# Wider value steps and single-element projections, a shorter inverse root, one more kept value tile an element, and a swapped softmax in a four-element transformer decode

## The chip, the cores and the metric

The kernel runs on one core of a Trainium2 chip. The metric is the time of one execution in device microseconds (us), lower is better. Single executions of this kernel differ by up to 4% on a busy chip, so each kernel is timed several times, alternating with the kernel before on the same chip.

## The reference, cut to what matters

Four batch elements, one query token each. Two identical layers, each attention over a cache of 4,096 keys and values, then a feed-forward network (FFN) with GELU. Both layers read the same key and value caches: 8 key/value heads of 4,096 x 128 in bf16, each serving 4 query heads.

```python
B, Sq, D = 4, 1, 512
Hq, Hkv, Sk, Dh = 32, 8, 4096, 128
F = 1792
x = x + attention(layernorm(x), k_cache, v_cache, wq, wo)
x = x + (gelu(layernorm(x) @ w_gate) * (layernorm(x) @ w_up)) @ w_down
# ... and the same two lines once more
```

Keys and values together are 67 MB for each sweep over all elements. The keys of an element stay on the chip from its first layer to its second; most value tiles have to be loaded twice.

## The kernel before

Elements are numbered 0 to 3. Each goes through the same round: key tiles (512 KB each) are loaded and scored, softmax runs on ScalarE and VectorE, value tiles pass through seven buffers, and a "dense stage" (output projection, FFN, query of the next layer) ends the element's first layer. The second layer's scores then free the key tiles, and the next element's keys are loaded into them. `vals.step()` is one value step: sixteen matmuls on one value tile, after which its buffer is free and the next load is issued.

```python
WIDE = 8                         # how often the four probabilities are streamed
...
# one value step: 4 neighbouring elements (the 4 query heads), repeated WIDE times
rhs = pe[:, s, c, :].unsqueeze(1).broadcast_to([P, WIDE, rep])
nc.tensor.matmul(self.ot[:, s % 2], lhsT=v[:, i, :], rhs=rhs, ...)
if last or (b, g, s, t) not in keep:
    free.append(held.pop((b, g, s, t)))
load_v()
...
# FFN down projection: ONE element (nb = 1), repeated n = 32 times
def down(nb, H_bf, between=()):
    n = WIDE * rep // nb
    y = ps_sm.tile([P, KD, n, nb], FP32, name="y", tag="sm")
    ...
            nc.tensor.matmul(y[:, k], lhsT=wd_sb[:, c, k * P:(k + 1) * P],
                             rhs=H_bf[:, c, :].unsqueeze(1).broadcast_to([P, n, nb]), ...)
    return y[:, :, 0]            # only the first copy is used
...
# projection of the last heads: one element, one column
nc.tensor.matmul(y[:, k], lhsT=wo_sb[:, i, k * P:(k + 1) * P], rhs=head_rhs(o_bf, i), ...)
...
# softmax and value steps at the start of an element's attention
p0 = soft(sc1)
vals.step(3)
soft_turn(p0)                    # VectorE transposes the probabilities
if not first:
    for i in range(2):
        out_proj(rows, OT_bf, heads[i], hp, i == 0)
pe, den = soft_swap(p0, p1p), soft_den(p0)     # TensorE turns them once more
...
# which value tiles stay on the chip for the second layer: some of element 0
keep = {(0,) + u[2:] for u in value_order(0, 1)[:KEEP]}
```

The repeated columns compute nothing new. They are there for TensorE's clock: in the first series below, doubling them in the value steps alone took the mean granted clock of the profiled run from 0.741 to 0.868.

## Time and profile before

| | kernel before |
|---|---|
| time, median of 3 runs | 308.94 us (307.83 to 309.42) |
| span of the profiled run | 306.7 us |
| data on the queue | 113.53 MB, busy 94.9% of the span |
| key loads start (elements 1, 2, 3), and the last refill of key tiles | 88.48, 146.78, 210.41, 274.34 us |
| mean granted TensorE clock | 0.741 |

From the profile's page: busy time of each engine, and the clock that was granted in 40 equal slices of the span, in tenths.

```profile
PE 202.7 (66%) x3865; PEld 119.6 (39%) x3873; DVE 172.6 (56%) x490; ACT 29.3 (10%) x71; POOL 0.7 (0%) x6
...
PEclk9999995556778559795976567889855585678675
```

No engine is busy all the time, and the clock changes between half (5) and full (9) about once a dense stage. The groups of instructions show the down projection, with its count, its busy time and the mean duration of one:

```profile
L356 PE MATMUL y<-H_bf,wd_sb 128*128 128x32 bf16 x280 | 9.6, 192 | 3.4 <-DVE H_bf L340 1.7
```

The durations of matmuls that follow each other overlap, so 192 ns is not the price of one. What a matmul costs in a dense sequence is the distance from one start to the next, which I computed from the trace for each group and each clock state. At full clock the down matmuls start 31 ns apart and the value matmuls, which stream as many columns, 25 ns apart.

### The profile page before, as it was taken

How to read it: one execution, taken by the hardware profiler on the slowest of the kernel's cores; microseconds unless marked ns; L12 is line 12 of the kernel's file. 1: busy time of each engine (PE TensorE's matmuls, PEld its weight loads, DVE VectorE, ACT ScalarE, POOL GpSimd, SP SyncE). 2: the span in 40 equal slices, each digit the busy share in tenths (PEclk: the TensorE clock that was granted, in tenths of full speed). 3: DMA queues.
4: the chain of work that ended last, by engine and by line, in shares of the span. 5: the costliest groups of instructions: out<-in, count | busy, mean ns of one | idle time of the engine just before them, and what ended most of it. 6: DMA issues, size and time to landing. Idle time of an engine off the chain costs nothing.

```text
span 306.7 us, 8771 instructions
## 1 busy us (share of the span) xinstructions
PE 202.7 (66%) x3865; PEld 119.6 (39%) x3873; DVE 172.6 (56%) x490; ACT 29.3 (10%) x71; POOL 0.7 (0%) x6
## 2 busy tenths in 40 slices
PE   1344385348786657889854379797563868997974
PEld 0011154122333134656431236474311455645654
DVE  6586831014358897365478944455598552555144
ACT  0003001000002021200100212000102040003000
POOL 0000000000000000000000000000000000000000
PEclk9999995556778559795976567889855585678675
DMA  6999999999959999999999999999999999999920
GB/s 253 431 409 426 410 420 412 358 377 387 394 154 361 400 413 417 417 416 414 350 392 412 414 419 368 345 412 417 416 405 412 419 416 416 377 307 410 414 86 3
DMA packets 34558, 114.09 MB, mean 372 GB/s; under 512 B 3156, under 2 KB 9048, under 8 KB 33496
## 3 DMA queue, kind: packets, MB, share of 16 engines
q1 hardware_dynamic: 34520, 113.53, 94.9%
q8 instruction: 30, 0.49, 0.6%
q14 instruction: 8, 0.07, 0.1%
HBM read 113.51 MB, written 0.00 MB: 370 GB/s over the span
## 4 chain that ended last, share of the span: by engine, by line
DMA 48%; PE 22%; DVE 16%; SPq 9%; issue 3%; ACT 2%; DVEq 0%; ACTq 0%
DMA kt<-in_A_k_cache_dram 25%; DMA v<-in_A_v_cache_dram 20%; PE sc L399 5%; PE ot L501 4%; DMA wd_sb<-in_B_w_down_dram 3%; SPq L140 3%; SPq L134 3%; DVE kt L388 3%; PE y L356 3%; DVE rows L223 2%; PE rows L314 2%; PE rows L233 2%; PE rows L288 2%; DVE pp L426 1%; ACT pp L418 1%
## 5 line engine op out<-in xcount | busy, mean ns | idle before, releaser
L388 DVE STREAM_TRANSPOSE kt<-kt 128x1024 f32<-128x1024 f32 x64 | 75.6, 1219 | 5.2 <-DMA kt<-in_A_k_cache_dram 5.0
L501 PEld LDWEIGHTS <-v 128*128 128x128 bf16 x1920 | 58.5, 100 | 51.0 <-DMA v<-in_A_v_cache_dram 26.5
L501 PE MATMUL ot<-pe,v 128*128 128x32 bf16 x1920 | 64.4, 182 | 20.8 <-DMA v<-in_A_v_cache_dram 18.4
L399 PE MATMUL sc<-kt,qb 128*32 128x512 bf16 x512 | 55.4, 491 | 19.3 <-DVE kt L388 15.7
L399 PEld LDWEIGHTS <-qb 128*32 128x32 bf16 x512 | 16.8, 108 | 44.8 <-issue 18.4
L223 DVE STREAM_TRANSPOSE rows<-rows 128x512 f32<-128x512 f32 (+1 forms) x23 | 16.2, 706 | 29.7 <-PE rows L233 12.9
L509 DVE TENSOR_TENSOR OT_bf<-ot,rden 128x8 bf16<-128x8 f32 (+1 forms) x40 | 6.5, 163 | 37.5 <-PE ot L501 37.2
L418 ACT ACTIVATE pp<-sc,nm 128x512 bf16<-128x512 f32 x16 | 11.0, 688 | 149.7 <-DVE junk L414 149.7
L445 PE MATMUL x<-pp,ident_bf 128*32 128x128 bf16 x256 | 7.8, 251 | 21.4 <-DVE pp L426 21.3
L288 PE MATMUL rows<-wo_sb,OT_bf 128*1 128x512 bf16 (+1 forms) x136 | 14.1, 508 | 7.4 <-DMA wo_sb<-in_A_wo_dram 6.3
L405 DVE TENSOR_REDUCE m<-sc 128x1 f32<-128x512 f32 x16 | 10.8, 677 | 12.6 <-PE sc L399 12.6
L233 PE MATMUL rows<-wq_sb,xn_bf 128*1 128x512 bf16 (+1 forms) x160 | 14.9, 503 | 4.4 <-DMA wq_sb<-in_A_wq_dram 4.1
L445 PEld LDWEIGHTS <-ident_bf 128*32 128x32 bf16 x256 | 5.8, 107 | 27.3 <-issue 24.5
L426 DVE STREAM_TRANSPOSE pp<-pp 128x512 bf16<-128x512 bf16 x16 | 11.2, 700 | 4.4 <-ACT pp L418 4.4
L356 PE MATMUL y<-H_bf,wd_sb 128*128 128x32 bf16 x280 | 9.6, 192 | 3.4 <-DVE H_bf L340 1.7
L254 PE MATMUL qe<-qm,t_bf 128*128 128x64 bf16 x16 | 3.3, 209 | 12.3 <-DVE qm L244 6.4
L448 ACT CAST pe<-x 128x512 bf16<-128x512 f32 x16 | 9.4, 586 | 19.9 <-PE x L445 19.9
L346 PE MATMUL sc<-wq_sb,ident_bf 128*128 128x512 bf16 x25 | 10.9, 511 | 0.2 <-issue 0.2
L356 PEld LDWEIGHTS <-wd_sb 128*128 128x128 bf16 x280 | 8.9, 100 | 4.7 <-DMA wd_sb<-in_B_w_down_dram 2.5
L257 DVE TENSOR_TENSOR qb<-qe,amask 128x256 bf16<-128x256 f32 x16 | 6.8, 424 | 4.6 <-PE qe L254 4.6
L301 DVE SCALAR_TENSOR_TENSOR XX<-XX,y 128x4 f32<-128x4 f32 x8 | 1.3, 158 | 13.3 <-PE y L356 9.4
L328 ACT ACTIVATE sq<-sq 128x14 f32<-128x14 f32 (+1 forms) x6 | 1.3, 219 | 76.0 <-DVE sq L326 76.0
(83 smaller groups left out, 135.8 us busy)
## 6 DMA issues: line engine op xcount, KB each, us to landing
v<-in_A_v_cache_dram SPq DMA_DIRECT2D x117, 512.0 KB, 8.0
kt<-in_A_k_cache_dram SPq DMA_DIRECT2D x48, 512.0 KB, 10.2
kt<-in_A_k_cache_dram SPq DMA_DIRECT2D x8, 1024.0 KB, 15.6
wq_sb<-in_A_wq_dram SPq DMA_DIRECT2D x2, 2048.0 KB, 13.9
wo_sb<-in_A_wo_dram SPq DMA_DIRECT2D x4, 1024.0 KB, 11.6
kt<-in_A_v_cache_dram SPq DMA_DIRECT2D x8, 512.0 KB, 10.1
wg_sb<-in_B_w_gate_dram SPq DMA_DIRECT2D x1, 1792.0 KB, 13.5
wu_sb<-in_B_w_up_dram SPq DMA_DIRECT2D x1, 1792.0 KB
```

Source lines behind the costliest of these rows:

```text
L223: nc.vector.transpose(out=rows[:, :n], in_=rows[:, :n])
L233: nc.tensor.matmul(rows[j * QS:j * QS + nb, :], lhsT=xn_bf[:, k, bs], rhs=w, start=(k == 0), stop=(k == KD - 1))
L288: nc.tensor.matmul(rows[r0:r0 + lhsT.shape[-1], :], lhsT=lhsT, rhs=wo_sb[:, i, :], start=(start and n < QD), stop=(stop and n >= hp - QD))
L346: nc.tensor.matmul(idle, lhsT=ident_bf[:, :], rhs=wq_sb[0][:, 0, :512], start=True, stop=True, skip_group_check=True)
L356: nc.tensor.matmul(y[:, k], lhsT=wd_sb[:, c, k * P:(k + 1) * P], rhs=H_bf[:, c, :].unsqueeze(1).broadcast_to([P, n, nb]), start=(c == 0 an ...
L388: nc.vector.transpose(out=words, in_=words)
L399: nc.tensor.matmul(sc[s * QS:(s + 1) * QS], lhsT=qb[:, w0:w0 + 2 * W], rhs=kt[:, :, be // 2, :, be % 2], start=(t == 0 and be == 0), stop= ...
L405: nc.vector.tensor_reduce(out=m[:], in_=sc.rearrange("p c j -> p (c j)"), axis=AX.X, op=ALU.max)
L418: nc.scalar.activation(out=pp[:], in_=sc[:], func=ACT.Exp, bias=nm[:, 0:1], scale=scale, accum_out=ls[:])
L426: nc.vector.transpose(out=flat, in_=flat)
L445: nc.tensor.matmul(x[a * QS:(a + 1) * QS, s], lhsT=ident_bf[:, s * QS:(s + 1) * QS], rhs=pT[:, a], start=True, stop=True, skip_group_check ...
L501: nc.tensor.matmul(self.ot[:, s % 2], lhsT=v[:, i, :], rhs=rhs, start=(c == 0), stop=(c == C - 1), skip_group_check=True)
```

## The change

Its intent: keep TensorE's clock up by streaming twice as many columns in value steps, and, of one element repeated, in the down projection and the last heads' projection; shorten the inverse root on VectorE that stands in the dense chain; keep one value tile of each of elements 1 to 3 on the chip (three loads fewer); let VectorE turn the second head group's probabilities earlier by moving value steps; fill the first dense stage with a few more idle matmuls.

```diff
-    WIDE = 8
+    WIDE = 16
...
+    magic1 = const.tile([P, 1], I32, name="magic1")
...
+    def ln_rstd_one(st):          # 8 instructions instead of 11
+        nc.vector.tensor_scalar(out=nv[:], in0=mean, scalar1=mean, scalar2=ex2, op0=ALU.mult, op1=ALU.subtract)
...
+            nc.vector.tensor_scalar(out=r2[:], in0=rstd[:], scalar1=rstd[:], scalar2=nh[:], op0=ALU.mult, op1=ALU.mult)
+            nc.vector.tensor_scalar(out=rstd[:], in0=r2[:], scalar1=1.5, scalar2=rstd[:], op0=ALU.add, op1=ALU.mult)
...
+    def widen(nb):
+        return WIDE * rep if nb == 1 else 1
...
-                                 rhs=head_rhs(o_bf, i), ...
+                                 rhs=rhs.broadcast_to([P, y.shape[2], y.shape[3]]), ...   # 1 column -> 64
...
     def down(nb, H_bf, between=()):
-        n = WIDE * rep // nb
+        n = widen(nb)                                                                     # 32 columns -> 64
...
-    keep = {(0,) + u[2:] for u in value_order(0, 1)[:KEEP]}
+    keep = {u[:1] + u[2:] for b in range(B) for u in value_order(b, 1)[:KEEP if b == 0 else 1]}
...
         p0 = soft(sc1)
-        vals.step(3)
         soft_turn(p0)
-        if not first:
-            for i in range(2):
-                out_proj(rows, OT_bf, heads[i], hp, i == 0)
+        vals.step(2)
         pe, den = soft_swap(p0, p1p), soft_den(p0)
+        prob1[gb] = (pe, soft_recip(den))
+        vals.step(8 - vals.n)
...
-            waits = iter((1, 5, 6, 2, 1, 0, 3, 1))
+            waits = iter((1, 5, 8, 5, 2, 1, 4, 2))
```

More of the change, by code (lines that the diff above doesn't have):

```diff
@@ L144, in build_consts @@
         nc.vector.memset(magic[:], 0x5F3759DF)
+        nc.vector.memset(magic1[:], 0x5F3759DF - 0x40400000)
         for r in ROWS:
@@ L173, in ln_center @@
         bs = slice(b0, b0 + nb)
-        mv = small.tile([P, 2, nb], FP32, name="mv", tag="mv")
         if nb == 1:
@@ L180, in ln_center @@
                                     scalar2=None, op0=ALU.subtract)
-            nc.vector.tensor_copy(out=mv[:], in_=st[:])
-            return mv
+            return st
+        mv = small.tile([P, 2, nb], FP32, name="mv", tag="mv")
         st = ps_sm.tile([P, 2, nb, KD], FP32, name="st", tag="sm")
@@ L189, in ln_center @@
         return mv
+    def ln_rstd_one(st):
+        mean, ex2 = st[:, 0], st[:, 1]
+        nv = small.tile([P, 1], FP32, name="nv", tag="nv")
+        nc.vector.tensor_scalar(out=nv[:], in0=mean, scalar1=mean, scalar2=ex2, op0=ALU.mult,
+                                op1=ALU.subtract)
+        nh = small.tile([P, 1], FP32, name="nh", tag="nh")
+        nc.vector.tensor_scalar(out=nh[:], in0=nv[:], scalar1=0.5, scalar2=-0.5 * LN_EPS,
+                                op0=ALU.mult, op1=ALU.add)
+        hv = small.tile([P, 1], I32, name="hv", tag="hv")
+        nc.vector.tensor_single_scalar(out=hv[:], in_=nh[:].bitcast(I32), scalar=1,
+                                       op=ALU.arith_shift_right)
+        rstd = small.tile([P, 1], FP32, name="rstd", tag="rstd")
+        nc.vector.tensor_tensor(out=rstd[:].bitcast(I32), in0=magic1[:], in1=hv[:],
+                                op=ALU.subtract)
+        r2 = small.tile([P, 1], FP32, name="r2", tag="r2")
+        for _it in range(2):
+            nc.vector.tensor_scalar(out=r2[:], in0=rstd[:], scalar1=rstd[:], scalar2=nh[:],
+                                    op0=ALU.mult, op1=ALU.mult)
+            nc.vector.tensor_scalar(out=rstd[:], in0=r2[:], scalar1=1.5, scalar2=rstd[:],
+                                    op0=ALU.add, op1=ALU.mult)
+        return rstd
     def ln_rstd(nb, mv):
+        if nb == 1:
+            return ln_rstd_one(mv)
         msq = small.tile([P, nb], FP32, name="msq", tag="msq")
@@ L270, in y_rows @@
         return yc
+    def widen(nb):
+        return WIDE * rep if nb == 1 else 1
     def y_select(yc, nb):
         t = yc.rearrange("p (k a) j -> p a k j", a=QD)
-        y = ps_sm.tile([P, KD, nb], FP32, name="y", tag="sm")
+        y = ps_sm.tile([P, KD, widen(nb), nb], FP32, name="y", tag="sm")
         for a in range(QD):
-            nc.tensor.matmul(y[a * QS:(a + 1) * QS], lhsT=s32_f[:, :], rhs=t[:, a],
+            nc.tensor.matmul(y[a * QS:(a + 1) * QS, :, 0], lhsT=s32_f[:, :], rhs=t[:, a],
                              start=True, stop=False, skip_group_check=True)
@@ L293, in out_proj_end @@
             for i in range(h0, h0 + hp):
+                rhs = head_rhs(o_bf, i).unsqueeze(1)
                 nc.tensor.matmul(y[:, k], lhsT=wo_sb[:, i, k * P:(k + 1) * P],
-                                 rhs=head_rhs(o_bf, i), start=False, stop=(i == h0 + hp - 1),
+                                 rhs=rhs.broadcast_to([P, y.shape[2], y.shape[3]]), start=False, stop=(i == h0 + hp - 1),
                                  skip_group_check=True)
@@ L596, in attend @@
         turn(5 if first else 1)
-        vals.step(2)
+        vals.step(2 if first else 1)
         sc1 = new_scores(0)
@@ L607, in attend @@
         p0 = soft(sc1)
-        vals.step(3)
         soft_turn(p0)
-        if not first:
-            for i in range(2):
-                out_proj(rows, OT_bf, heads[i], hp, i == 0)
+        vals.step(2)
         pe, den = soft_swap(p0, p1p), soft_den(p0)
+        prob1[gb] = (pe, soft_recip(den))
+        vals.step(8 - vals.n)
         if two:
+            out_proj(rows, OT_bf, heads[0], hp, True)
             p1 = soft(sc2[1])
-        prob1[gb] = (pe, soft_recip(den))
         vals.step(3)
@@ L619, in attend @@
             soft_turn(p1)
+            out_proj(rows, OT_bf, heads[1], hp)
             pe1, den1 = soft_swap(p1, p2p), soft_den(p1)
@@ L630, in attend @@
             return (y, OT_bf, heads[3], hp), vals2
+        vals.step(2)
+        out_proj(rows, OT_bf, heads[2], hp)
         vals.step()
         keep_clock(1)
-        vals.step()
-        out_proj(rows, OT_bf, heads[2], hp)
-        vals.step()
         out_proj(rows, OT_bf, heads[4], rep, False, True)
@@ L688, in dense @@
         out_proj_end(*proj)
-        y = proj[0]
+        y = proj[0][:, :, 0]
         fill(1)
@@ L713 @@
             fill = prev.step
-        dense(b, 1, proj, fill, {KF // 2: 1, KF - 4: 1} if prev is None else ())
+        dense(b, 1, proj, fill, {KF // 2: 1, KF - 4: 1, KF - 1: 2} if prev is None else ())
         ln_square(b, 1)
@@ L745 @@
     out_proj_end(*proj)
-    add_y(0, B, proj[0])
+    add_y(0, B, proj[0][:, :, 0])
     ln_square(0, B)
```

## The prediction

> **What bounds the kernel now.** I read the DMA rows of the page first, then the busy table of chosen stretches, the queue's waits, and the timeline of one dense stage.
>
> ```profile
> DMA  6999999999959999999999999999999999999920
> GB/s 253 431 409 426 410 420 412 358 377 387 394 154 361 400 413 417 417 416 414 350 392 412 414 419 368 345 412 417 416 405 412 419 416 416 377 307 410 414 86 3
> ...
> q1 hardware_dynamic: 34520, 113.53, 94.9%
> ```
>
> The transfers are the first bound: the one queue is busy 94.9% of the span. Most of the 40 slices move 410 to 420 GB/s, which is this kernel's full rate; the last two are nearly empty.
>
> ```profile
> 26.00:54.00 28.00, 15.76 (x319) 10.35 (x319) 14.65 (x25) 4.42 (x9) 0.00 (x0) 0.87 1.02 415
> 84.00:94.00 10.00, 8.31 (x93) 2.81 (x87) 5.51 (x19) 1.09 (x3) 0.00 (x0) 0.77 0.59 175
> ...
> 146.00:156.00 10.00, 6.49 (x131) 3.50 (x123) 4.73 (x13) 1.67 (x4) 0.00 (x0) 0.95 1.00 348
> ...
> 188.00:198.00 10.00, 8.01 (x212) 5.99 (x214) 3.58 (x17) 1.12 (x4) 0.00 (x0) 0.91 0.93 328
> ...
> 264.00:276.00 12.00, 11.34 (x251) 7.01 (x239) 6.22 (x31) 0.21 (x1) 0.00 (x0) 0.77 0.97 323
> ...
> 293.00:307.00 14.00, 7.57 (x230) 6.72 (x230) 6.32 (x34) 0.45 (x2) 0.00 (x0) 0.60 0.03 10
> ```
>
> Columns: stretch, its length, each engine's busy time, granted clock, DMA share, GB/s. At 415 GB/s a 512 KB tile takes 1.26 us. Against 415, the stretch from 84 loses (415-175)/415 x 10 = 5.8 us, that from 146 loses 1.6, from 188 2.1, from 264 2.7: 12.2 us in which the queue could have moved more. The last 14 us are a tail without transfers.
>
> Where the losses come from: in each of elements 1 to 3 the key tiles can be refilled only when the scores of the layer before have read them, and that comes at the end of a dense stage (projection, FFN, query). I followed issues and landings in the trace. Key loads start at 88.48 and 146.78 and 210.41; the same point for the last element (values into the freed key tiles) is 274.34. The last two rounds take 63.6 and 63.9 us. One round is 16 key and 32 value tiles, 25.17 MB, 60.6 us at 415 GB/s: about 3 us per round is not transfer. The round is a loop: last value tile lands, dense chain, key loads, key tiles, value tiles. During the chain only the seven value buffers feed the queue.
>
> ```profile
> SPq L479 <- PE ot L501: 70.4, 63, 2.9
> ```
>
> ```profile
> DMA to landing us min/median/max: 5.3/8.0/22.2
> ```
>
> A value load waits 70.4 us in total for TensorE to free a buffer, and is never on the chip in under 5.3 us; where it takes about 8, the queue is full, where it takes 5 to 6.5 the queue had run shallow and I find the gaps in the landings (1.8 to 2.8 us between two tiles where 1.24 is normal). Seven buffers are 7 x 1.26 = 8.8 us of transfers, six are 7.5: only just above the latency.
>
> The chain of element 3, on TensorE:
>
> ```profile
> 258.44 0.63 PE L501 MATMUL ot<-pe,v 128*128 128x32 bf16 x16 [0.22 <-issue]
> ...
> 261.38 1.66 PE L314 MATMUL rows<-wg_sb,xn_bf 128*1 128x448 bf16 x16
> ...
> 263.52 1.66 PE L314 MATMUL rows<-wu_sb,xn_bf 128*1 128x448 bf16 x16
> ...
> 269.42 1.88 PE L233 MATMUL rows<-wq_sb,xn_bf 128*1 128x512 bf16 x16
> ...
> 273.24 1.09 PE L399 MATMUL sc<-kt,qb 128*32 128x512 bf16 x16
> ```
>
> From its last value step (258.44) to the first freed keys (274.34) it takes 15.9 us; 16.0 for element 2 (194.39 to 210.41) and 15.4 for element 1. The clock is 0.50 for the gate, up and first query matmuls here: 1.66, 1.66 and 1.88 us. At 0.95 the same sets take 0.95 and 1.09 (elements 1 and 2).
>
> ```profile
> 141.25 0.24 DVE L179 TENSOR_SCALAR xn_bf<-XX,st 128x4 bf16<-128x4 f32 x1 [0.74 <-PE st L177]
> 141.40 0.15 DVE L181 COPY mv<-st 128x2 f32<-128x2 f32 x1
> ...
> 143.32 0.16 DVE L208 SCALAR_TENSOR_TENSOR rstd<-r,rstd 128x1 f32<-128x1 f32 x1
> ...
> 143.51 0.23 DVE L723 TENSOR_SCALAR am<-amask,rstd 128x4 f32<-128x4 f32 x1
> 143.65 0.73 DVE L223 STREAM_TRANSPOSE rows<-rows 128x512 f32<-128x512 f32 x1
> ```
>
> From the centred row to the root's result VectorE needs 143.48 - 141.40 = 2.08 us in 11 small instructions, and the query's transpose waits for it.
>
> ```profile
> L501 PE MATMUL ot<-pe,v 128*128 128x32 bf16 x1920 | 64.4, 182 | 20.8 <-DMA v<-in_A_v_cache_dram 18.4
> L399 PE MATMUL sc<-kt,qb 128*32 128x512 bf16 x512 | 55.4, 491 | 19.3 <-DVE kt L388 15.7
> ```
>
> **What the Trainium skill says.** "TensorE: Matmul & The Clock Gate", Part 1: a free-running window of about 3.4 us of activity decides between half and full clock. The trace agrees in kind: states of 0.5 and 0.949 in multiples of 3.41 us. Counting streamed columns per window, those under about 2,600 are followed by 0.50 and those over about 3,100 mostly by 0.95. The same page, "Back-to-back issue gap": N/1.2 ns cold, N/2.4 + 2.5 warm, with a floor near 25 ns. The value matmuls start every 26 to 28 ns at 0.5 and every 25 at 0.95; so 32 columns cost the floor when warm, and 64 should cost 53 cold and about 29 warm (estimate from that page; no 64-column stream is in this trace). "VectorE: DVE Perf Modes", the TRN2 errata: a fixed cost per instruction that small operands do not shrink. It agrees: 128x1 operations take 153 to 159 ns; tensor_scalar with a pointer scalar takes 229 to 236. "DMA: Bandwidth & Descriptors", Specifications: a fabric ceiling of 435 GB/s; 415 sustained is near it, so only fewer bytes or fewer gaps help.
>
> **The change part by part.**
>
> *64 columns.* 2,048 value matmuls and 224 of the single-element down projections, and 80 of the last heads' projections (1 column before). Cold, a value step of 16 grows from 0.43 to 0.85 us; warm by 0.03 to 0.06. A cold dense stage would lose 10 x 0.42 plus 56 x 22 ns = 5.4 us. But a step now streams 1,024 columns instead of 512: at one tile per 1.26 us that is 2.7 steps, 2,800 columns a window, near the boundary by itself, and with the dense matmuls (1,792 for a gate set) well over it. So I expect the dense stages warm. Worth: gate and up each 0.7 shorter, query 0.8, first scores 0.4, statistics 0.2. Not all is on the chain: in element 3 the gate's transpose waits for VectorE's root (ends 263.27) whatever the clock; there the gain is about 0.6 at up, 0.2 at the statistics, and about 1 at the end of attention, where out-projection, idle matmuls and row turning run cold between 253 and 258. Element 1: 0.6 (scores, statistics). Element 2: 0.4 to 0.8. Sum about 2.4 us.
>
> *Inverse root.* 11 instructions become 8: one with two pointers from PSUM (0.24), two with immediates (0.31), one integer subtract (0.16), four with pointers (0.92), and 7 gaps of 0.037: 1.89 us, against 2.08. The count falls by 27% but the pointer forms are dearer: 0.2 us each. Two per element on the chain, six or eight in all: 0.8 us after overlaps.
>
> *Kept tiles.* Three loads of 512 KB fewer: 126 value loads become 123, 3 x 1.26 = 3.8 us of transfer. The price: one of seven buffers is held from the last steps of element b's first layer through its dense stage, just where the queue runs shallow. Each of the 12 value loads in between is issued one step later; the four behind them are not. The queue has one tile fewer to bring before the keys, which helps only if the keys are already asked for: element 2 had 6.8 us of values outstanding when the keys were asked (217.19 - 210.41), element 1 5.1, element 3 6.3. Less 1.26, all lie at 3.9 to 5.5, under the latency. I count two thirds: 2.5 us.
>
> *Softmax swapped.* Element 2: its value steps at 181.61, 182.85 and 184.06 wait for tiles; VectorE's turn of the probabilities stands behind their outputs and runs at 184.79 although ScalarE was done at about 183.4, 16 cold out-projections follow, and no buffer is freed from 184.7 to 188.2. The landings then thin out (196.12 comes 2.0 after 194.09), and steps of the dense stage wait at 196.16 and 197.38. With the turn ahead of the steps and two steps behind the swap, buffers come free more evenly. Worth about 1.0 us in element 2, little elsewhere; a smaller pool takes some back: 0.8.
>
> *First dense stage.* More idle matmuls. Two before the last down chunk and one more before the statistics stand on the path: 0.3 to 0.6 us warm. In exchange 81 to 88 should run at 0.95: scores 1.57 to 0.9, statistics 0.56 to 0.36. Query matmuls gain nothing, since VectorE's root ends later. Net 0.3 us off the 84 to 94 gap.
>
> Sum: 2.4 + 0.8 + 2.5 + 0.8 + 0.3 = 6.8; 308.94 - 6.8 = 302.1, I say 302.2. The tail does not change: its matmuls stay 1 to 4 columns wide and its root is the old one (down 0.1 us cheaper).
>
> **The rivals.** (1) *The smaller pool eats the kept tile.* For it: the latencies of 5.3 to 6.5 us at elements 1 and 3 with all seven buffers. Against: the keys then move up by as much. Then no gain from keeping and 1 to 2 us lost: about 305.5. (2) *The clock stays cold.* For it: windows follow what TensorE gets to do, and from the first key tile on it idles for 15 us, so values begin cold. Against: cold 64-column steps fill 0.85 of 1.26 us, which by itself lifts the next window. If dense stages were cold anyway, 4 to 5 us each: about 315. (3) *The round becomes purely transfer-bound.* With a chain of 14.5 us and even frees, 47 tiles take 59.3 us a round: three rounds save 4.3 each, 13 in all with nothing lost: about 296. Against: restarting key loads from a shallow queue cost 2.7 us between the first two tiles after 88.48.
>
> **Range and chances.** Between (1) and half of (3): 298.0 to 306.5. The 2% mark is 308.94/1.02 = 302.9, close to my middle, so faster 0.53, same 0.44; slower needs (2): 0.03.
>
> **What would show it.** Right: the value matmuls start 27 to 31 ns apart in the dense stages and PEclk is 0.95 there; about 111.9 MB on the queue; VectorE's root at about 1.9 us; rounds of about 61.5 us between key issues; no gap in value frees where element 2's was. Wrong: value loads landing 5 to 6 us after issue with landings 2 us apart through the dense stages (rival 1); starts 53 ns apart at 0.50 there (rival 2); 415 GB/s right through 146 to 290 (rival 3).

## The result, and the profile after

The changed kernel took 317.45 us (median of 4 runs, 316.6 to 319.1); the kernel before took 309.18 us (median of 4 runs, 307.83 to 310.08) on the same chip. The ratio is 1.0278, with a 95% interval of 1.0219 to 1.0336: slower, where the prediction had it faster. All ratios here are the mean time of one kernel's fast runs over that of the other's of the same rounds, so not quite the ratio of the medians that are quoted. A run counts as fast when it is within 1.5% of the fastest of its kernel; because that cut depends on one run, I give the medians of all runs beside the ratios.

The page of the changed kernel, same rows as before:

```profile
PE 217.6 (69%) x3884; PEld 142.8 (45%) x3884; DVE 172.4 (54%) x467; ACT 29.4 (9%) x71; POOL 0.7 (0%) x6
...
PEclk9999997758999758999958778979975679999995
DMA  7999999999949999999999999978999999989920
GB/s 243 424 415 423 404 409 388 349 386 378 379 128 393 404 410 403 350 406 333 337 414 409 410 404 282 387 281 284 359 412 411 407 408 398 401 282 382 410 76 3
...
q1 hardware_dynamic: 34088, 111.96, 92.7%
```

The clock did what was hoped: far more nines, a mean of 0.869 against 0.741. The 1.57 MB of the three kept tiles are gone from the queue. Yet the span of the profiled run is 317.3 us, 10.6 more. Two things are to be seen in the GB/s row: valleys of 281 to 284 GB/s in slices 25, 27 and 28 (element 2's round), and slices that are full but mostly hold 404 to 412 where the kernel before mostly held 412 to 419 (its GB/s row stands in the prediction). The second looked like nothing at first.

The same stretches of the kernel, at its own times (columns as in the prediction):

```profile
26.00:54.00 28.00, 17.29 (x309) 12.73 (x308) 14.51 (x26) 4.63 (x9) 0.00 (x0) 0.94 1.02 408
86.00:96.00 10.00, 7.34 (x100) 2.92 (x93) 6.01 (x20) 1.09 (x3) 0.00 (x0) 1.00 0.52 164
150.00:160.00 10.00, 6.94 (x131) 3.91 (x132) 3.74 (x13) 1.67 (x4) 0.00 (x0) 0.94 1.00 345
...
274.00:286.00 12.00, 10.72 (x211) 7.93 (x207) 5.45 (x25) 0.00 (x0) 0.00 (x0) 1.00 0.89 317
```

These stretches run at 0.94 to 1.00 of the clock, and still move no more data than before. The one cold spot in a dense stage of this run is in element 2, from 206.6 to 210 us. The prediction's count of streamed columns, redone on this trace, agrees with the clock: all 49 windows of 3.41 us with over 3,100 columns are followed by the full clock (26 of 27 in the kernel before; matmuls into 32 array columns or fewer count a quarter).

Where the 10.6 us lie follows from the first key load of each element. They start at 90.40, 151.05, 219.84, and the last refill at 284.12. So 1.9 us are lost until the first; the three rounds between take 60.65, 68.79 and 64.28 us against 58.30, 63.63 and 63.93, that is 7.9 us; and 0.8 us come after the last. Within a round, the chain from the last value step before the projection to the freed keys takes 16.88, 20.01 and 16.88 us against 15.42, 16.02 and 15.90.

TensorE's timeline shows what lengthened the chain. The kernel before, element 1 (start, length, instruction, how many, and in brackets what ended the idle time before it):

```profile
132.17 0.54 PE L294 MATMUL y<-OT_bf,wo_sb 128*128 128x1 bf16 x16 [0.25 <-DVE OT_bf L509]
...
138.19 1.91 PE L356 MATMUL y<-H_bf,wd_sb 128*128 128x32 bf16 x56 [0.92 <-DVE H_bf L340]
```

The changed kernel, elements 1 and 3:

```profile
135.07 1.09 PE L323 MATMUL y<-OT_bf,wo_sb 128*128 128x64 bf16 x16 [0.25 <-DVE OT_bf L538]
...
139.81 1.19 PE L530 MATMUL ot<-pe,v 128*128 128x64 bf16 x32
141.52 3.40 PE L385 MATMUL y<-H_bf,wd_sb 128*128 128x64 bf16 x56 [0.52 <-DVE H_bf L369]
...
270.57 0.93 PE L343 MATMUL rows<-wg_sb,xn_bf 128*1 128x448 bf16 x16
...
272.01 0.93 PE L343 MATMUL rows<-wu_sb,xn_bf 128*1 128x448 bf16 x16
...
274.59 3.41 PE L385 MATMUL y<-H_bf,wd_sb 128*128 128x64 bf16 x56 [0.34 <-DVE H_bf L369]
```

The gate and up matmuls of element 3 (L343) are at 0.93 us, from 1.66: the clock works. But the down projection of an element (a "set" of 56 matmuls) takes 3.40 us, from 1.91, at that same full clock. Fifty-six matmuls of about 0.2 us each, overlapping, in 3.40 us are (3.40 - 0.2) / 55 = 58 ns from start to start. The value matmuls between them, also 64 columns, need 1.19 us for 32, which is 31 ns each. The heads' projection shows the same 58 ns, where one column took 25 to 27.

The swap shows on TensorE too. The kernel before, element 2, where the probabilities (L445) follow the out-projection:

```profile
184.06 0.61 PE L501 MATMUL ot<-pe,v 128*128 128x32 bf16 x16 [0.65 <-DMA v<-in_A_v_cache_dram]
184.60 1.88 PE L288 MATMUL rows<-wo_sb,OT_bf 128*1 128x512 bf16 x16
186.26 0.64 PE L445 MATMUL x<-pp,ident_bf 128*32 128x128 bf16 x16
```

The changed kernel at the same place:

```profile
185.72 1.28 PE L530 MATMUL ot<-pe,v 128*128 128x64 bf16 x32
188.90 0.41 PE L474 MATMUL x<-pp,ident_bf 128*32 128x128 bf16 x16 [1.90 <-DVE pp L455]
```

In these traces TensorE starts its matmuls in the order of its list: no value matmul starts between 187.0 and 189.48 us. With only two value steps ahead of the probabilities' matmuls it stands idle for 1.90 us until VectorE has turned them, and no buffer is freed meanwhile. Before, out-projection work filled that time. The loads are late after it, and SyncE's wait for TensorE to free value buffers is longer (70.4 us in the kernel before):

```profile
SPq L508 <- PE ot L530: 77.5, 61, 3.6
```

### The profile page after: what moved, and what is told of

Its sections match the earlier page's. It is cut to its first block, busy times and chain, and to the rows that moved or that the text cites.

```text
span 317.3 us, 8771 instructions
## 1 busy us (share of the span) xinstructions
PE 217.6 (69%) x3884; PEld 142.8 (45%) x3884; DVE 172.4 (54%) x467; ACT 29.4 (9%) x71; POOL 0.7 (0%) x6
## 4 chain that ended last, share of the span: by engine, by line
DMA 51%; PE 25%; DVE 15%; SPq 5%; issue 3%; ACT 1%; DVEq 0%; ACTq 0%
DMA v<-in_A_v_cache_dram 22%; DMA kt<-in_A_k_cache_dram 21%; PE ot L530 8%; DMA wd_sb<-in_B_w_down_dram 5%; PE y L385 5%; PE sc L428 4%; SPq L135 3%; DMA kt<-in_A_v_cache_dram 3%; DVE kt L417 3%; DVE rows L248 2%; PE rows L316 1%; DVE pp L455 1%; DVE r L208 1%; ACT pp L447 1%; SPq L136 1%
## 5 line engine op out<-in xcount | busy, mean ns | idle before, releaser
L530 PEld LDWEIGHTS <-v 128*128 128x128 bf16 x1920 | 75.3, 106 | 40.6 <-issue 21.7
L530 PE MATMUL ot<-pe,v 128*128 128x64 bf16 x1920 | 83.2, 205 | 11.5 <-DMA v<-in_A_v_cache_dram 10.0
L428 PE MATMUL sc<-kt,qb 128*32 128x512 bf16 x512 | 50.6, 453 | 18.6 <-DVE kt L417 16.7
L428 PEld LDWEIGHTS <-qb 128*32 128x32 bf16 x512 | 15.8, 102 | 41.8 <-issue 17.5
L316 PE MATMUL rows<-wo_sb,OT_bf 128*1 128x512 bf16 (+1 forms) x136 | 12.7, 445 | 7.4 <-DMA wo_sb<-in_A_wo_dram 7.0
L385 PE MATMUL y<-H_bf,wd_sb 128*128 128x64 bf16 (+1 forms) x280 | 15.7, 208 | 2.2 <-DVE H_bf L369 1.7
L385 PEld LDWEIGHTS <-wd_sb 128*128 128x128 bf16 x280 | 14.8, 99 | 3.4 <-DVE H_bf L369 1.1
L258 PE MATMUL rows<-wq_sb,xn_bf 128*1 128x512 bf16 (+1 forms) x160 | 12.4, 433 | 4.5 <-DMA wq_sb<-in_A_wq_dram 4.4
L375 PE MATMUL sc<-wq_sb,ident_bf 128*128 128x512 bf16 x44 | 14.0, 411 | 0.0
L330 DVE SCALAR_TENSOR_TENSOR XX<-XX,y 128x4 f32<-128x4 f32 x8 | 1.3, 159 | 22.0 <-PE y L385 15.4
L477 ACT CAST pe<-x 128x512 bf16<-128x512 f32 x16 | 9.4, 586 | 24.8 <-PE x L474 15.4
L465 DVE RECIPROCAL rden<-den 128x16 f32<-128x16 f32 x16 | 4.0, 250 | 9.1 <-PE den L460 8.6
```

The costliest lines, as they stand in the source:

```text
L258: nc.tensor.matmul(rows[j * QS:j * QS + nb, :], lhsT=xn_bf[:, k, bs], rhs=w, start=(k == 0), stop=(k == KD - 1))
L316: nc.tensor.matmul(rows[r0:r0 + lhsT.shape[-1], :], lhsT=lhsT, rhs=wo_sb[:, i, :], start=(start and n < QD), stop=(stop and n >= hp - QD))
L375: nc.tensor.matmul(idle, lhsT=ident_bf[:, :], rhs=wq_sb[0][:, 0, :512], start=True, stop=True, skip_group_check=True)
L428: nc.tensor.matmul(sc[s * QS:(s + 1) * QS], lhsT=qb[:, w0:w0 + 2 * W], rhs=kt[:, :, be // 2, :, be % 2], start=(t == 0 and be == 0), stop= ...
```

## The experiments

Eighteen kernels ran, all with correct results. The kernel before ran beside them on the same chip, with medians of 309.14, 308.35, 306.79, 306.97 and 308.43 us in the five series. Each series had another chip, so across series the ratios are to be compared, not the medians. Edits longer than a few lines are given in words, and some expectations count the elements from 1. The first theory was that a matmul of 64 single-element columns costs 57 ns at the full clock, where 29 was forecast, and that this is nearly all of the loss. Its rivals were that the swap's stall is the cause, that the smaller value pool is, and that wider value steps are.

### First series: the single columns

**The changed kernel with the narrow projections.** Everything as changed except:

```diff
 def widen(nb):
-    return WIDE * rep if nb == 1 else 1
+    return 1                      # heads' projection: one column
 def down(...):
-    n = widen(nb)
+    n = 8 * rep // nb             # down: 32 columns
```

> The changed kernel, but the down projection streams 32 columns again and the last heads' projection one; the value steps keep 64. Theory 1 (the repeated single column is slow: 57 ns a matmul at the high clock where 29 was forecast): down falls from 57 to about 31 ns, the projection to 25, each element's chain gets about 2 us shorter, and the kernel runs in 309 to 311 us. Rival (the new order of the softmax and the kept tile cost it all): within 2 us of the changed kernel, 315 to 317 us.

Measured: 309.01 us (median of 20 runs), ratio 1.0052 (1.0012 to 1.0091). Undoing these two widths takes 8.4 us off 317.45, or 2.3% by the ratios. What remains of the change is level with the kernel before by the medians and half a per cent slower by the ratio: its other five parts together gain nothing.

**The changed kernel with 64 down columns from four neighbours.** The hidden vector is written four times side by side, so the 64 columns read four equal neighbouring elements sixteen times over; the heads' projection is at one column.

```diff
-    H_bf: [P, KF, nb]             rhs = one element, repeated 64 times
+    H_bf: [P, KF, 4]              rhs = four equal elements, repeated 16 times
```

> The changed kernel with the projection at one column, and the down projection still at 64 columns, but taken from four equal neighbours repeated 16 times, as the value steps' columns are, in place of one element repeated 64 times. If the slow thing is the repetition of one element, down falls to 28 to 31 ns and the time is that of the run before it or a little less. If 64 columns into this accumulator are slow whatever is read, down stays at 57 ns and the time is about 6 us longer than that run.

Measured: 310.31 us (median of 4 runs), ratio 1.0101 (1.0000 to 1.0202). In the down projection the width is 64 and the arithmetic is the same as in the changed kernel; only the places read differ. The time can't be told from that of the run before it. A set now takes 1.89 us instead of 3.40:

```profile
142.56 1.89 PE L390 MATMUL y<-H_bf,wd_sb 128*128 128x64 bf16 x56
```

That is 31 ns, the same as a value matmul. So 64 columns are not dear; 64 columns of one element are.

**The kernel before with only these two widths.**

```diff
+def widen(nb): return 64 if nb == 1 else 1      # used in y_select, out_proj_end, down
```

> The kernel before with only the down projection and the last heads' projection at 64 columns. Theory 1: down takes 57 ns at the high clock (53 at the low one) where it took 31 (27), so 1.4 us an element, and the projection 0.5 us an element and 1 us in the first: 314 to 316 us in all. Rival: the cost came from something else, 308 to 310 us.

Measured: 313.47 us (median of 4 runs), ratio 1.0149 (1.0020 to 1.0278); only two of the four runs count as fast. The chains are 17.2 to 17.4 us instead of 15.4 to 16.0, and the sets are as in the changed kernel:

```profile
139.48 3.40 PE L360 MATMUL y<-H_bf,wd_sb 128*128 128x64 bf16 x56 [1.04 <-DVE H_bf L344]
```

In this profile a part of the down matmuls falls into the half clock, and they start 58 ns apart there too, where 53 had been expected. This part alone makes the kernel slower. It is 4.3 us by the medians here, where the run above gave 8.4; the interval, up to 2.8%, holds both.

**The kernel before with only the value steps at 64 columns.**

```diff
-    self.ot = ps_ot.tile([P, 2, WIDE, rep], ...)        # WIDE = 8
+    self.ot = ps_ot.tile([P, 2, 16, rep], ...)
```

> The kernel before with only the value steps at 64 columns. Forecast's own reasoning: higher clock in the dense stages at 28 to 31 ns a value matmul there, 2 us gained: 305 to 308 us. Rival (64 columns cost more than they warm, since the value phases start cold at 53 ns): 310 to 313 us.

Measured: 306.74 us (median of 12 runs), ratio 0.9991 (0.9953 to 1.0028). In its profile all three chains take 15.06 us, 0.7 less than before on average, and the value matmuls start 31 ns apart at full clock and 53 at half. This part does what was forecast for it in the chain; in time it is level by the ratio, 2.4 us better by the medians.

### Second series: the other parts alone

**Only the swap.**

```diff
 soft_turn(p0)
+vals.step(2)
 pe, den = soft_swap(p0, p1p), soft_den(p0)      # and the other moves of the change
```

> The kernel before with only the new order of softmax and value steps in the attention of elements 1 to 4's first layer. The forecast gave it 0.8 us of gain. Rival: TensorE works in order, so with the swap's 16 matmuls after only two value steps it stands still until VectorE has turned the probabilities (2.5 us in the changed kernel's trace between value steps 57 and 58, with tiles landed), the buffers come free late and the queue runs shallow: 1 to 3 us slower, 310 to 312 us against 309, most of it between the key loads and the last value step of the next element (42.9, 47.6, 48.0 us before), and some 1 us before the first weights.

Measured: 312.51 us (median of 22 runs), ratio 1.0074 (1.0038 to 1.0111); by the medians it is 4.2 us, because half of its runs do not count as fast. The stalls are there without any other part (the kernel before waits 1.27 us at the first of these two places and not at all at the second; over the whole run this group waits 26.5 us for VectorE, 21.3 before):

```profile
46.51 0.62 PE L445 MATMUL x<-pp,ident_bf 128*32 128x128 bf16 x16 [2.02 <-DVE pp L426]
...
187.34 0.62 PE L445 MATMUL x<-pp,ident_bf 128*32 128x128 bf16 x16 [2.14 <-DVE pp L426]
```

**Only the kept tiles.**

```diff
-keep = {(0,) + u[2:] for u in value_order(0, 1)[:KEEP]}
+keep = {u[:1] + u[2:] for b in range(B) for u in value_order(b, 1)[:KEEP if b == 0 else 1]}
```

> The kernel before with only one value tile of elements 2 to 4 kept (1.57 MB less to read). The forecast gave it 2.5 of 3.8 us. Rival 1 of the forecast (one buffer fewer through the dense stage eats it): no gain, value loads landing 5 to 6 us after their issue and dense chains a little longer than 15.4, 16.0 and 15.9 us, time 308 to 310 us.

Measured: 305.28 us (median of 6 runs), ratio 0.9886 (0.9838 to 0.9934): 3.1 to 3.5 us gained of the 3.8 us of transfers saved. In this kernel the smaller pool does not eat the kept tile.

**Only the root.**

```diff
+magic1 = const.tile([P, 1], I32, name="magic1")
 def ln_rstd(nb, mv):
+    if nb == 1:
+        return ln_rstd_one(mv)
```

> The kernel before with only the shorter inverse root. Forecast: 0.2 us a time, 0.8 us in all. From the changed kernel's trace (tensor_scalar with two pointers 273 ns, with one 214): 0.1 us a time on VectorE, 0.3 us or less in all, which these rounds can't tell from none: 308.5 to 309.5 us.

Measured: 310.70 us (median of 22 runs), ratio 1.0092 (1.0060 to 1.0125). Slower, although the root's own chain in the trace is 0.1 us shorter: 1.97 us against 2.08. This had no explanation at the time.

**All parts but the swap and the single columns.**

```diff
+value steps of 64 columns
+ln_rstd_one and magic1
+keep one tile of each of elements 1 to 3
+idle matmuls of the first dense stage
```

> The changed kernel without the two parts suspected: single columns streamed 32 and 1 wide as before, softmax in the old order. It keeps the 64-column value steps, the root, the kept tiles and the idle matmuls. If the wide single columns and the order were the whole loss, and the forecast's sizes for the rest hold (2.4 + 0.8 + 2.5 + 0.3), 303 to 304.5 us; if the kept tiles bring nothing, 306 to 307 us; if it is no faster than before, one of the parts left costs time as well.

Measured: 307.81 us (median of 22 runs), ratio 0.9999 (0.9967 to 1.0031). Its chains are the shortest so far, 14.81 to 14.85 us, 0.6 to 1.2 us less than before in each of three elements, and one finds nothing of it in the time.

### Third series: pairs of parts

**Value steps and root.**

```diff
+value steps of 64 columns
+ln_rstd_one and magic1
```

> The kernel before with 64-column value steps and the shorter root, nothing else. The root alone measured 310.7 us against 308.35 of the kernel before (medians), although the profile of it shows chains of waits no longer than before; 64-column value steps alone measured 306.74 against 309.14. Theory A, the root itself costs the chain (two-pointer forms of 273 to 280 ns, the row's statistics held in PSUM longer): about 1.0 us above the kernel before's median less 2.4 plus 2.4, so level with it, ratio 0.998 to 1.004. Theory B, the root is harmless and its 2.4 us was an accident of how the transfers fell out: about 2.4 us below the kernel before or a little more, ratio 0.988 to 0.993. In both, VectorE's root takes 1.98 us from the centred row to the result.

Measured: 310.55 us (median of 6 runs), ratio 1.0123 (1.0068 to 1.0177). Neither theory had that much; it speaks against a harmless root.

**Value steps and kept tiles.**

```diff
+value steps of 64 columns
+keep one tile of each of elements 1 to 3
```

> The kernel before with 64-column value steps and the kept tiles of elements two to four, nothing else: the two parts that gained alone (medians -2.4 and -3.1 us). Theory A, they add up: 5.5 us below the kernel before, some 303 us, ratio 0.980 to 0.984, which beats both kernels. Theory B, they share one gain (both only help the queue reach the keys sooner, and the six buffers left are the limit with either): 3 to 4 us below, ratio 0.987 to 0.991. If the kept tile costs more with wider steps, the ratio is above 0.992.

Measured: 307.53 us (median of 14 runs), ratio 1.0023 (0.9982 to 1.0065). A miss: neither the sum nor half of it came, only the third branch, a ratio above 0.992. Its profiled run is the fastest of the fourteen, so the profile doesn't show what the others lose. The kept tile, worth 1.1% alone, is worth nothing beside the wider value steps in this series.

**Value steps, kept tiles and root.**

```diff
 value steps of 64 columns, kept tiles
+ln_rstd_one and magic1
```

> The run with 64-column value steps and kept tiles, and the shorter root as well. If the root itself costs (theory A of the run with value steps and root): 2 to 2.4 us above the run without it, so near 305 to 306 us. If it is harmless: within 1 us of the run without it. Against the earlier run that has these three parts and the added idle matmuls of the first dense stage (307.81 us, against 308.35 before): if the idle matmuls cost nothing, this run is as far below the kernel before as that one, 0.5 us; if this run is 2 us or more lower than that, the idle matmuls cost that.

Measured: 307.45 us (median of 14 runs), ratio 1.0010 (0.9975 to 1.0045), level with the run above. Here the root does no harm. It also differs from the second series' last kernel only by the idle matmuls of the first dense stage: 1.0010 without, 0.9999 with them, so those are neutral, as far as two chips can be compared.

**The changed kernel with the old order of softmax and value steps.**

```diff
 changed kernel; single columns stay at 64
-vals.step(2) ahead of soft_swap, out-projections behind it
+vals.step(3) ahead of soft_turn, out-projections ahead of soft_swap
```

> The changed kernel with the old order of softmax and value steps, all else as changed (the 64 single columns in the down projection and the heads' projection stay). The same kernel with the narrow down projection and the old order was 307.81 us; the single columns alone cost 4.3 us on the kernel before, but 8.4 us within the changed kernel (317.45 against 309.01). Theory A, the single columns cost by their own time in the chain, 2 us an element: about 314 to 316 us, and the swap then adds 1 to 3. Theory B, half of their cost within the changed kernel comes from the swap's stalls, which leave no value step in reserve to cover a longer chain: about 311 to 312.5 us.

Measured: 314.70 us (median of 6 runs), ratio 1.0253 (1.0192 to 1.0314). The narrow counterpart is the second series' last kernel, at 0.9999. So without the swap the single columns cost 2.5%, with it 2.3% (1.0278 against 1.0052): no dependence of the two on each other is to be seen, and what the swap adds inside the changed kernel is 0.3 to 0.5%. The chains are 16.85 us against 14.83 with narrow columns. That is 2.02 us, and the sets account for all of it: 56 x (58 - 31) + 16 x (58 - 26) ns = 1.51 + 0.51 = 2.02.

### Fourth series: what sets the 58 ns

**128 single columns in the down projection** (one look, state unknown).

```diff
-    n = widen(nb)                 # 64
+    n = 128                       # heads' projection: one column
```

> The changed kernel with 128 single columns in the down projection, and one column again in the heads' projection. Theory A, each column of one repeated element takes 0.9 ns whatever the clock (32 columns: 31 ns at the full clock; 64: 58): the down matmuls start 115 to 116 ns apart, a set of 56 takes 6.5 us, and the chain from the last value step to the keys is 3.2 us longer than with 64. Theory B, they stream at the clock's rate after a fixed loss of about 30 ns: [...]86 ns when warm, 107 to 137 when cold.

Measured: 327.30 us, against a median of 306.97 before. The matmuls start 111 ns apart at full clock:

```profile
145.03 6.38 PE L385 MATMUL y<-H_bf,wd_sb 128*128 128x128 bf16 x56
```

With 31, 58 and 111 ns for 32, 64 and 128 columns, each column more costs 0.83 ns. The rival's 86 ns is out. I had put 0.9 ns; 0.83 ns is the slope, and it equals the rate of the value matmuls in the half state: 53 / 64. What in the reading of one place sets it, no view shows.

**64 columns from two neighbours** (one look, state unknown).

```diff
-    H_bf: [P, KF, nb],  rhs = one element x 64
+    H_bf: [P, KF, 2],   rhs = two equal elements x 32     (heads' projection: one column)
```

> The changed kernel with 64 columns in the down projection from two equal neighbours, 32 times over, and one column in the heads' projection. Theory A, the loss goes with stepping back to the same place after each element, so two neighbours (4 bytes) halve it: about 31 ns at the full clock, as with four neighbours. Theory B, only runs of four or more (8 bytes) stream at the full rate: between 40 and 58 ns.

Measured: 309.34 us, and again 31 ns: a pair of neighbours, 4 bytes, is enough.

```profile
141.23 1.89 PE L390 MATMUL y<-H_bf,wd_sb 128*128 128x64 bf16 x56
```

**Single columns in the down projection alone.**

```diff
 def widen(nb):
-    return WIDE * rep if nb == 1 else 1
+    return 1                      # heads' projection: one column
 def down(...):
-    n = widen(nb)
+    n = 64 if nb == 1 else 1      # down: 64 single columns, as changed
```

> The changed kernel with 64 single columns in the down projection as changed, and one column in the heads' projection as before. The changed kernel was 8.4 us above the one with both narrow. By their time in the trace, the down projection's 56 matmuls grow by 27 to 31 ns each, 1.5 us an element, the heads' projection's 16 by 31 to 33, 0.5 us: of 2 us an element the down projection has three quarters. So some 6 us above the kernel with both narrow, which was level with the kernel before to 0.5% above it: ratio 1.018 to 1.026. If the heads' projection has more of it (it comes at the start of the chain, where the queue is still fed): the same or higher; if it has most: below 1.012.

Measured: 314.70 us (median of 4 runs), ratio 1.0255 (1.0196 to 1.0314), the upper end of what was expected. The down projection has most of the loss: three quarters by the sets (1.51 of 2.02 us), and four runs can't tell three quarters from all.

**Kept tiles, and a 32-column down projection from four neighbours.**

```diff
 kernel before + keep line
-    rhs = one element x 32
+    rhs = four equal elements x 8
```

> The kernel before with the kept tiles of elements two to four (3.1 us below before when alone), and the 32 columns of its own down projection read from four equal neighbours instead of one. Theory A, a repeated single element costs 0.9 ns a column also at 32 columns: the down matmuls fall from 31 to 25 ns at the full clock, 0.3 us an element; in all 3 to 4.4 us below the kernel before, ratio 0.986 to 0.990. If the kept tile's gain was an accident of that series, the ratio is 0.995 or above.

Measured: 305.44 us (median of 11 runs), ratio 0.9923 (0.9891 to 0.9956). A gain comes in a second series too, though smaller than expected (0.5% by the medians), and how much of it is the kept tiles' this run can't say. The down matmuls are at 25 ns, so even the kernel before paid the price of single columns, 6 ns each:

```profile
137.45 1.57 PE L361 MATMUL y<-H_bf,wd_sb 128*128 128x32 bf16 x56 [0.47 <-DVE H_bf L343]
```

### Fifth series: why the root cost time

In all profiles of kernels with the new root the last weights land later than in the kernel before (81.9 to 82.5 us against 81.2), with a delay that begins before a single new root has run, and I then saw that their full slices in the GB/s row are lower. The root brings a constant, a tile of four bytes a partition.

**The constant alone.**

```diff
+    magic1 = const.tile([P, 1], I32, name="magic1")
+    nc.vector.memset(magic1[:], 0x5F3759DF - 0x40400000)      # nothing reads it; the root is the old one
```

> The kernel before with the root's added constant (one tile of 4 bytes a row and one memset), which nothing reads; the root is the old one. Theory A, the loss of the root runs comes from where that tile moves others: slower by 0.6 to 1.0%, ratio 1.005 to 1.010, and the last weight tile of the first stage lands at about 82.2 us instead of 81.2 to 81.7. Theory B, it comes from the root's instructions: level with the kernel before, ratio 0.996 to 1.004, weights at 81.2 to 81.7.

Measured: 309.29 us (median of 22 runs), ratio 1.0069 (1.0036 to 1.0103). By the ratio a tile that nothing reads makes the kernel 0.7% slower; by the medians it is 0.3%. Its row of rates:

```profile
GB/s 243 430 410 425 405 409 405 352 372 392 383 180 321 408 409 408 407 406 382 383 409 407 407 408 406 407 397 386 379 405 406 408 409 405 401 366 410 406 71 3
```

**The root without a tile of its own.** The constant is a fifth column of a tile that is there already, and the intermediate results use the old root's tiles.

```diff
-    magic  = const.tile([P, B], I32, name="magic")
-    magic1 = const.tile([P, 1], I32, name="magic1")
+    magic  = const.tile([P, B + 1], I32, name="magic")
```

> The kernel before with the shorter root, but its constant is a fifth column of a tile that is there already and its intermediate results use the old root's tiles. Theory A, where tiles lie: level with the kernel before or 0.2 us faster, ratio 0.994 to 1.002. Theory B, the instructions: slower as the root alone was, ratio 1.006 to 1.012, and the weights land at about 82.2 us.

Measured: 307.12 us (median of 22 runs) against 308.43 before, ratio 1.0022 (0.9989 to 1.0054): level. Set against each other, with 22 runs each on one chip, the run with the tile has a median 2.2 us longer than this one. Its full slices are back at 413 to 419, and the last weights land at 81.6 us instead of 82.1:

```profile
GB/s 246 425 416 420 414 421 412 357 378 387 396 145 362 394 416 416 419 415 414 397 404 384 410 402 353 331 414 418 414 408 411 413 411 381 387 347 404 414 69 3
```

Over all twenty profiles, the mean of the ten best slices from the thirteenth on is 413.5 to 416.7 GB/s in the eight kernels without the tile and 408.1 to 409.7 in the twelve with it, with none between. The queue's packets say the same: three quarters of the 4 KB packets take at most 159 ns without it, and 164 to 165 ns with it. That the tile does it is shown; the added write to it is not the cause, since the last run has one more too. How is not: I suppose that it shifts the places of the tiles that the transfers write to, but no view shows these places, and four bytes more a partition can't be it as such, since the last run has them as well.

## Why the prediction was wrong

**The step that failed** is the price of a matmul: "so 32 columns cost the floor when warm, and 64 should cost 53 cold and about 29 warm". It was read off value matmuls, and the part on the 64 columns then applied it to "2,048 value matmuls and 224 of the single-element down projections, and 80 of the last heads' projections" alike. It holds for the value matmuls, which read four neighbours: 53 and 31 ns. For one repeated element the runs showed 58 ns, at the full clock and at half. At 31 to 58 ns for the down projection and 26 to 58 for the heads' projection an element's chain grows by 2.0 us. Three chains and the first dense stage (7.78 us from the last weights to the keys against 6.86, in the pair with the old order that differs only in these columns) make 7.0 us by the profiles, and 6.9 to 8.4 us by the times of the two such pairs. That is most or all of the 8.3 us lost. The prediction's sum has no term for these columns when warm; it charged them only in a cold stage. The profile before had the hint in it: 31 ns against 25 at 32 columns and full clock.

**The clock** was right. The dense stages are warm but for 3.4 us in element 2, gate and up of the last element shrank from 1.66 to 0.93 us, the chain with wide value steps alone is 0.7 us shorter in each element, some 2.2 us in all, though the ratio of that kernel shows no gain in time (0.9991). That 2.2 comes near the forecast's 2.4 is partly luck: the terms that the forecast lists (1.8, 0.6 and 0.4 to 0.8) make 2.8 to 3.2. Rival (2), at about 315 us, resembles the outcome only in the number: its cause, dense stages cold throughout with starts of 53 ns, did not occur. (The forecast's sum for a cold stage takes 22 ns a down matmul, 53 less 31; in the half state the down matmuls had been 27 ns apart, so 26 would fit.)

**The inverse root** was mis-sized and hid a cost. 1.89 us was forecast and 1.97 measured, because the instructions with two pointers take 273 to 282 ns where 230 to 240 had been put; those with one take 214. Nothing is left of the 0.8 us: level without its tile. The tile, which the prediction passed over entirely, costs 0.3 to 0.7% alone, and all kernels built from the changed one carry it.

**The kept tiles** were right in sign and undersized: 2.5 us counted, 3.1 to 3.5 measured alone (1.5 to 2.4 in the other series, with four neighbours as well). So rival (1) is refuted for that part alone. It gained nothing beside wider value steps, which is open.

**The swap** had the wrong sign. The forecast expected evenly freed buffers. It looked at when VectorE could start, not at what TensorE has to do until VectorE is done; with the out-projections moved behind, it stands for 1.6 to 2.2 us at four places where it stood for 0 to 1.3 before. Alone that costs 0.7% by the ratio and 1.3% by the medians, within the changed kernel 0.3 to 0.5%.

**The first dense stage** is neutral, where 0.3 us had been forecast. Rival (3), a round bound by transfers alone, did not occur: the dense stages still move only 164 to 345 GB/s, and the full rate itself fell by 1.7%. Its 296 us was miscounted, too: it saves 4.3 us in each of three rounds of 59.3 us, but the first round already took 58.3.

So the sum of the other parts, where 6.8 us of gain had been forecast, is at most 1% slower than the kernel before (1.0052, interval 1.0012 to 1.0091). The single columns are the loss on top. How the parts cancel is not shown, and two things stay open. The parts do not add up over the series: value steps with kept tiles should have gained, and the root with value steps alone should have lost less. And the profiled run of the changed kernel has a chain of 20.01 us in element 2, in which the up matmuls ran cold (1.67 us) and value tiles landed up to 2.8 us apart although they had been asked for more than 8 us earlier; the queue moved 379 to 418 GB/s from 200 to 206 us, so it was not short of work there. The stall at 187 us lies just before it, but only one profile shows it. The kernel with only the kept tiles beats both kernels, at 0.9886 of the time of the one before; the one with four neighbours as well has 0.9923.

## What to carry to other kernels

Price a matmul by what it reads, not only by its width: time one group of the same read pattern from start to start in the trace you have, and where a moving operand repeats one element, write it twice side by side. Before moving work out of an in-order engine's list, ask what it does in that time instead. And after any change that adds a tile, compare the rate of the full slices with before: a tile that nothing reads can cost more than the shorter code it came for saves.

## What the Trainium skill lacked or had wrong

- "TensorE: Matmul & The Clock Gate", section "Back-to-back issue gap", gives N/2.4 + 2.5 ns for an isolated warm matmul and warns of the weight loads at small N, but has nothing on what the moving operand reads. With the same weight loads the runs show 31 ns for 64 columns of two or four neighbours (29 by the formula), but 31, 58 and 111 ns for 32, 64 and 128 columns of one repeated element at full clock: 0.83 ns a column, the page's cold rate.
- "SBUF — State Buffer", section "Operand start alignment", says of its own measurements that they are about legality and that "these runs timed nothing". Here one unread tile of 4 bytes a partition lowered the full rate of the transfers from about 416 to about 408 GB/s, and the time went up by 0.3% (medians) to 0.7% (ratio). Whether it is a matter of alignment no run here shows.
- "VectorE: DVE Perf Modes", section "Scalar operands", gives no cost for scalars that are read through a pointer. On 128x1 operands the runs show 153 ns with immediates, 214 ns with one pointer, and with two 273 ns, or 282 where they are read from PSUM.
